# A spectral mixer and token MLP on one core: contiguous chunked filter loads, one product op per unit, the even and odd inverse at once, statistics on two engines

## The chip, the cores and the metric

The kernel runs on one core of a Trainium2 chip. The metric is device time in microseconds (us); lower is better. "Span" is the time from the first to the last instruction in a profile; it is about 1.7 us shorter than the time. A run is called slow when it lies over 1.5% above the fastest of the same kernel; comparisons below use fast runs, and where a slow profile is shown the text says so.

## The reference, cut to what matters

```
x: [1, 2048, 512] bf16;  w_r, w_i: [2048, 257];  w1: [2048, 1376];  w2: [1376, 2048]
h  = x + irfft2( rfft2(layernorm(x)) * (w_r + i*w_i) )     # 2D transform over sequence and width
n  = layernorm(layernorm(h))                               # over the width
u  = gelu(n^T w1 + b1)                                     # an MLP over the sequence (token mixing)
y  = h + (u w2 + b2)^T
```

The kernels compute the transforms as matmuls with constant matrices. Stage by stage: statistics of the 16 row tiles of x and scaling of the forward matrix (FS); first forward matmul and its eviction (Y); second and third forward matmul (CS and a PSUM tile); product with the filter (V); two inverse matmuls (PQ, EO and a PSUM tile); sum with x (H); normalisation (HH); first MLP matmul (HH, weights W1); GELU (GT); second MLP matmul (weights W2); output. The filter takes 4.2 MB in the layout that the product needs: 128 partitions hold 32 groups of 257 values for each of w_r and w_i, used in eight units of four groups. Half of the partitions need rows in rising order ("plain"), the other half in falling order ("mirrored").

## The kernel before

A small scheduler in the program orders all operations and derives the semaphore waits. It finds dependencies by memory cells of 32 bytes:

```python
CELL = 32
...
        b = lo + offs * esz
        c = np.unique(np.concatenate([b // CELL, (b + esz - 1) // CELL]))
        quads = range(p0 // 32, (p0 + pn - 1) // 32 + 1)
        return [q * 16384 + int(x) for q in quads for x in c]
```

The filter is loaded in three chunks of groups. A row is 257 x 2 = 514 bytes, so that chunk borders (byte 4112, for example) fall inside a 32-byte cell:

```python
    for g0, g1 in ((0, 8), (8, 16), (16, 32)):
        n = (g1 - g0) * 257
        for w, dram in ((0, A_w_r), (1, A_w_i)):
            d = Wx[w][0:64, g0:g1, :]                                   # plain half, two copies
            dma(..., d, bass.AP(dram.tensor, g0 * 257, [[0, 2], [64 * 257, 32], [1, n]]), ..., outs=[d], prio=28)
            ...                                                         # one more row for group 0, also [[0, 2], ...]
            for comp in range(2):                                       # mirrored half
                d = Wx[w][64 + comp * 32:96 + comp * 32, h0:g1, :]
                dma(..., d, bass.AP(dram.tensor, (64 - h0) * 257, [[64 * 257, 32], [-257, g1 - h0], [1, 257]]), ..., outs=[d], prio=28)
```

The product takes two VectorE ops of 1024 elements per unit, one for each filter part. The last inverse matmul builds even plus odd and even minus odd in PSUM with three matmuls (512 + 256 + 256 columns), and one VectorE op adds x:

```python
        mm(f"g3_{s2}_e", ..., IF[:, s2, 0, :], ev2, unit, True, False, True, 8, 512, ...)
        for h in range(2):
            mm(f"g3_{s2}_o{h}", ..., IF[:, s2, h, :], EO[:, s2, 256:512], unit, False, h == 1, False, 8, 256)
        K.op(f"h_{s2}", "dve", ... tensor_tensor(hs, ps[:, bank, :], xs, ALU.add) ...)
```

Statistics are VectorE's (`bn_stats` and `bn_aggr`, 16 tiles for each of two normalisations), the scaling of the forward matrix is shared by Pool and ScalarE, and the GELU is a chain of six ops over ScalarE and VectorE.

## Time and profile before

| | us |
|---|---|
| time, median of 3 runs (range) | 206.91 (206.56 to 207.19) |
| start to last forward eviction Y | 0 to 25.4 |
| second forward matmul, filter wait, products, to the start of the inverse | 25.4 to 109.3 |
| inverse and first MLP matmul | 109.3 to 162.6 |
| second MLP matmul, output, end | 162.6 to 205.2 |

The page of the profile cuts the span into 40 slices of 5.1 us. A digit is the busy share of an engine in tenths (9 is 90% or more); PEclk is the granted clock of TensorE in tenths; GB/s is what the DMA engines moved. Then follows the chain of waits, traced back from the last instruction:

```profile
PE   0087599100000000058858999999999999999992
PEclk9999969855555555558997999999999999999999
DMA  5931511414999332326997000000000001211111
GB/s 170 364 159 48 127 51 58 115 46 136 309 412 431 71 90 69 82 55 195 353 285 272 2 0 0 3 0 0 0 2 3 0 26 54 74 53 53 51 51 53
...
PE 44%; SPq 35%; DVE 8%; DMA 8%; issue 2%; ACT 1%; DVEq 0%
PE ps L521 44%; SPq L516 35%; DMA Wi<-in_A_w_i_dram 8%; DVE V L665 7%; DVE OUT L755 0%; ACT U_58 L739 0%; ACT SG_61 L745 0%; ACT PQ L527 0%; SPq L515 0%; DVE Q_59 L741 0%; DVE P_60 L744 0%; DVE GT L747 0%; DVE Q_59 L742 0%; DVEq L421 0%
```

TensorE has nothing to do for nine slices. In six of these the DMA engines are mostly idle too, at 46 to 136 GB/s; in the three between (309, 412 and 431 GB/s) they are full. SPq L516 in the chain is SyncE issuing loads. The timeline of TensorE shows the hole exactly (start, length, instruction, and in brackets the idle time before it):

```profile
36.88 0.61 PE L521 MATMUL ps<-CS,EM 64*128 64x256 bf16 x8 [0.57 <-ACT CS L527]
82.78 0.37 PE L521 MATMUL ps<-EM,V 128*128 128x128 bf16 x2 [45.29 <-DVE V L665]
89.34 1.68 PE L521 MATMUL ps<-EM,V 128*128 128x128 bf16 x14 [6.19 <-DVE V L665]
```

The windows view gives busy time per engine in chosen stretches, then the clock, the DMA share and GB/s (a share can pass 1, because the view counts a packet wholly in the stretch where it starts):

```profile
core 0: us, PE busy (x) PEld busy (x) DVE busy (x) ACT busy (x) POOL busy (x), PEclk, DMA share, GB/s
30.00:33.00 3.00, 3.00 (x30) 2.31 (x29) 0.00 (x0) 2.77 (x5) 0.00 (x0) 1.00 0.12 52
41.00:48.00 7.00, 0.00 (x0) 0.00 (x0) 0.00 (x0) 0.00 (x0) 0.00 (x0) 0.50 0.13 48
60.00:65.00 5.00, 0.00 (x0) 0.00 (x0) 0.00 (x0) 0.00 (x0) 0.00 (x0) 0.50 1.01 425
```

A DMA share of 0.12 to 0.13 is what two of sixteen engines would give (2/16 = 0.125). The packets in the trace fit: from 41 to 48 us nearly all bytes go in packets of 8224 bytes that take 311 ns (median), so that two engines would carry 53 GB/s, beside 48 measured; two packets are in flight for 97% of that stretch, against 16 for 87% of the stretch from 60 to 65 us. (The packed trace does not name the engine of a packet: "two engines" below is read from these numbers.) The timeline of SyncE shows in which order it issued, and how long an issue held it:

```profile
22.31 15.52 SPq L516 DMA_DIRECT2D Wi<-in_A_w_i_dram  x3
37.87 10.72 SPq L516 DMA_DIRECT2D IF<-c_IF  x1
48.64 2.18 SPq L516 DMA_DIRECT2D W_77<-in_B_w_dram  x4
50.86 0.44 SPq L515 DMA_DIRECT2D B1s<-in_B_b_dram  x1
51.34 18.63 SPq L516 DMA_DIRECT2D B2s<-in_B_b_dram  x1
70.01 3.43 SPq L516 DMA_DIRECT2D Wr<-in_A_w_r_dram  x3
...
87.61 0.81 SPq L516 DMA_DIRECT2D Wi<-in_A_w_i_dram  x2
```

The filter rows of the first unit are partly among those issued at 70 us, behind the inverse matrix (IF) and all first MLP weights (W_77): 6.6 MB.

### The profile page before, as it was taken

To read this page: it belongs to the slowest core of one execution; us is meant where nothing else is said; L and a number is where in the kernel's file an instruction comes from. 1 tells how busy PE (TensorE), PEld (TensorE's weight loads), DVE (VectorE), ACT (ScalarE), POOL (GpSimd) and SP (SyncE) were. 2 spreads that over 40 slices of the span, in tenths; PEclk is the share of its full clock that TensorE was granted. 3 is DMA by queue.
4 is the path that set the end of the run, shared out by engine and by line. 5 is a ranking of instruction groups with operands and counts; after the bars stand their busy time and mean duration, and the time that the engine had idled before them with its cause. 6 is when DMAs were issued, how large, how long until landed. Compare 5 with 4: busy or idle time off the path is not lost.

```text
span 205.2 us, 2060 instructions
## 1 busy us (share of the span) xinstructions
PE 129.1 (63%) x775; PEld 77.8 (38%) x784; DVE 87.8 (43%) x199; ACT 72.0 (35%) x128; POOL 7.8 (4%) x14
## 2 busy tenths in 40 slices
PE   0087599100000000058858999999999999999992
PEld 0054346000000000036545665544444566666661
DVE  2787000000000001169992999996885442223321
ACT  2269969400000000024445897646963310000000
POOL 0056200000000000000000000000000000000000
PEclk9999969855555555558997999999999999999999
DMA  5931511414999332326997000000000001211111
GB/s 170 364 159 48 127 51 58 115 46 136 309 412 431 71 90 69 82 55 195 353 285 272 2 0 0 3 0 0 0 2 3 0 26 54 74 53 53 51 51 53
DMA packets 11834, 22.18 MB, mean 108 GB/s; under 512 B 2384, under 2 KB 8528, under 8 KB 11056
## 3 DMA queue, kind: packets, MB, share of 16 engines
q1 hardware_dynamic: 11824, 22.05, 32.4%
q8 instruction: 6, 0.10, 0.2%
q14 instruction: 4, 0.03, 0.0%
HBM read 19.95 MB, written 2.10 MB: 107 GB/s over the span
## 4 chain that ended last, share of the span: by engine, by line
PE 44%; SPq 35%; DVE 8%; DMA 8%; issue 2%; ACT 1%; DVEq 0%
PE ps L521 44%; SPq L516 35%; DMA Wi<-in_A_w_i_dram 8%; DVE V L665 7%; DVE OUT L755 0%; ACT U_58 L739 0%; ACT SG_61 L745 0%; ACT PQ L527 0%; SPq L515 0%; DVE Q_59 L741 0%; DVE P_60 L744 0%; DVE GT L747 0%; DVE Q_59 L742 0%; DVEq L421 0%
## 5 line engine op out<-in xcount | busy, mean ns | idle before, releaser
L521 PE MATMUL ps<-EM,V 128*128 128x128 bf16 x128 | 12.7, 247 | 55.2 <-DVE V L665 54.5
L521 PE MATMUL ps<-HH,W_77 128*128 128x512 bf16 (+1 forms) x171 | 39.9, 379 | 0.3
L521 PEld LDWEIGHTS ps<-EM,V 128*128 128x128 bf16 x128 | 9.2, 111 | 59.2 <-issue 46.2
L527 ACT ACTIVATE PQ<-ps 128x512 bf16<-128x512 f32 x16 | 8.9, 596 | 62.3 <-PE ps L521 62.0
L521 PEld LDWEIGHTS ps<-HH,W_77 128*128 128x128 bf16 (+1 forms) x176 | 17.4, 100 | 18.0 <-ACT HH L593 0.5
L727 DVE CAST B2f<-B2s 128x16 f32<-128x16 bf16 x1 | 0.2, 174 | 53.6 <-DMA B2s<-in_B_b_dram 53.6
L755 DVE SCALAR_TENSOR_TENSOR OUT<-ps,B2f,H 128x512 bf16<-128x512 f32 x16 | 12.0, 751 | 24.2 <-PE ps L521 24.2
L521 PE MATMUL ps<-FS,X 128*128 128x256 bf16 x64 | 10.1, 316 | 13.6 <-POOL FS L610 12.7
L521 PEld LDWEIGHTS ps<-FS,X 128*128 128x128 bf16 x64 | 6.7, 113 | 16.7 <-POOL FS L610 13.5
L665 DVE TENSOR_TENSOR V<-ps,Wi 128x1024 bf16<-128x1024 f32 x8 | 9.8, 1225 | 6.7 <-DMA Wi<-in_A_w_i_dram 6.4
L579 DVE BATCH_NORM_STATS2 st_93<-X 128x6 f32<-128x512 bf16 x16 | 10.5, 671 | 5.0 <-DMA X<-in_A_x_dram 5.0
L715 DVE TENSOR_TENSOR H<-ps,X 128x512 bf16<-128x512 f32 x16 | 10.6, 662 | 4.4 <-PE ps L521 4.4
L665 DVE TENSOR_TENSOR V<-ps,Wr 128x1024 bf16<-128x1024 f32 x8 | 9.7, 1216 | 6.1 <-DMA Wr<-in_A_w_r_dram 6.1
L579 DVE BATCH_NORM_STATS2 st_98<-H 128x6 f32<-128x512 bf16 x16 | 11.0, 690 | 0.2
L527 ACT ACTIVATE CS<-ps 128x512 bf16<-128x512 f32 x16 | 10.3, 791 | 2.3 <-PE ps L521 2.1
L521 PE MATMUL ps<-EM,Y 128*128 128x256 bf16 x64 | 10.0, 302 | 1.4 <-ACT Y L527 1.4
L593 ACT ACTIVATE HH<-H,nb_102,rs_101 128x512 bf16<-128x512 bf16 x12 | 9.7, 811 | 3.3 <-DVE nb_102 L591 3.3
L527 ACT ACTIVATE EO<-ps 128x512 bf16<-128x512 f32 x16 | 9.2, 588 | 2.9 <-PE ps L521 2.7
L521 PE MATMUL ps<-EM,PQ 128*128 128x256 bf16 x64 | 9.7, 289 | 0.7 <-ACT PQ L527 0.7
L521 PE MATMUL ps<-EO,IF 128*128 128x256 bf16 (+1 forms) x48 | 9.6, 308 | 0.1
L527 ACT ACTIVATE Y<-ps 128x1024 bf16<-128x1024 f32 x8 | 7.9, 1022 | 1.8 <-PE ps L521 1.7
L610 POOL TENSOR_SCALAR FS<-FP,rs_96 128x256 bf16<-128x256 bf16 x8 | 7.4, 924 | 14.2 <-ACT FP L598 9.3
(71 smaller groups left out, 177.9 us busy)
## 6 DMA issues: line engine op xcount, KB each, us to landing
W_77<-in_B_w_dram SPq DMA_DIRECT2D x4, 1376.0 KB, 18.8
out_dram<-OUT SPq DMA_DIRECT2D x16, 128.0 KB, 1.8
X<-in_A_x_dram SPq DMA_DIRECT2D x3, 512.0 KB, 8.2
Wr<-in_A_w_r_dram SPq DMA_DIRECT2D x4, 257.0 KB, 21.5
Wi<-in_A_w_i_dram SPq DMA_DIRECT2D x4, 257.0 KB, 22.7
IF<-c_IF SPq DMA_DIRECT2D x1, 1024.0 KB, 21.9
EM<-c_EM SPq DMA_DIRECT2D x1, 768.0 KB, 10.3
Wr<-in_A_w_r_dram SPq DMA_DIRECT2D x1, 514.0 KB
```

Of the source, the lines that this page charges most:

```text
L516: return eng.dma_start(dst, src)
L521: return eng.matmul(outf(bank), lhsT, rhs, start=start, stop=stop, **({"skip_group_check": True} if skip else {}))
L527: return eng.activation(dst, srcf(bank), ACT.Copy)
L579: K.op(f"ln{which}_st{i}", "dve", lambda s, eng, bank: eng.bn_stats(st[:, i, 0:6], src), ins=[src], outs=[st[:, i, 0:6]], dur=680.0, prio= ...
L593: K.op(f"ln{which}_ap{i}", "act", lambda s, eng, bank: eng.activation(dst, src, ACT.Identity, bias=c, scale=b), ins=[src, b, c], outs=[dst ...
L610: return eng.tensor_scalar(FS[:, :, i, :], FP[:, :, i, :], rs, None, op0=ALU.mult)
L665: return eng.tensor_tensor(ov, src, wv, ALU.mult)
L715: K.op(f"h_{s2}", "dve", lambda s, eng, bank, xs=xs, hs=hs: eng.tensor_tensor(hs, ps[:, bank, :], xs, ALU.add), ins=[xs], outs=[hs], dur=6 ...
L727: K.op("b2f", "dve", lambda s, eng, bank: eng.tensor_copy(B2f[:, :], B2s[:, :]), ins=[B2s[:, :]], outs=[B2f[:, :]], dur=80.0)
L755: K.op(f"fin{s2}", "dve", lambda s, eng, bank, dst=dst, bia=bia, hs=hs: eng.scalar_tensor_tensor(dst, ps[:, bank, :], bia, hs, op0=ALU.add ...
```

## The change

The intent: load the filter in five chunks in the order of use, each load with 32 rows outermost; do the product of a unit in one op; let one inverse matmul give even and odd parts and form sum and difference on VectorE; give ScalarE a part of the statistics; use ScalarE's own GELU. The core of the diff, cut:

```diff
-CELL = 32
+CELL = 4
 ...
-    for g0, g1 in ((0, 8), (8, 16), (16, 32)):
-            dma(f"ld_w{w}p_{g0}", d, bass.AP(dram.tensor, g0 * 257, [[0, 2], [64 * 257, 32], [1, n]]), 64 * n * 2, outs=[d], prio=28)
+    for ch, (u0, u1) in enumerate(((0, 1), (1, 2), (2, 4), (4, 6), (6, 8))):
+                d = W[comp::4, g0:g0 + ng, w, :]          # every fourth partition; no outs, the product waits by after=wload[u]
+                lst.append(dma(f"ld_wp{ch}_{w}{comp}", d, bass.AP(dram.tensor, g0 * LW, [[64 * LW, 32], [LW, ng], [1, LW]]), ...
 ...
-        for w in range(2):                                 # two products of 1024 per unit
+            s = bass.AP(s.tensor, s.offset, [list(s.ap[0]), [256, 4], [0, 2], [1, 256]])   # one of 2048, PSUM read twice
+            return eng.tensor_tensor(vout, s, win, ALU.mult)
 ...
-        mm(f"g3_{s2}_e", ...); for h in range(2): mm(f"g3_{s2}_o{h}", ...)
+        mm(f"g3_{s2}", lambda bank: ps[:, bank, :], IF[:, s2, :], EO[:, s2, :], unit, True, True, True, 8, 512)
+        dve(f"tl_{s2}", ... tt[:, 0, :] = ps[256:512] + xl); dve(f"th_{s2}", ... tt[:, 1, :] = xh - ps[256:512])
+        dve(f"h_{s2}", ... hs = ps[0:256] (read twice) + tt)
 ...
+STAT_ACT = (3, 7, 10, 13)                                  # tiles whose statistics ScalarE computes with accumulators
+FS_ACT = (13, 14, 15)                                      # tiles that ScalarE scales, Pool the other 13
 ...
-        gelu{t}_u, _q, _p, _in, _sg, _g                    # six ops
+        act(f"gelu{t}", GT[0:Mt, t, :], ..., ACT.Gelu_apprx_tanh, ...)
```

Also: forward evictions of 512 instead of 1024 elements, the second normalisation with ScalarE's Square and an accumulator, loads of the forward matrix from ScalarE's queue, and a final wait on two stores' semaphores instead of all.

## The prediction

> **What bounds the kernel now.** One hole. In the timeline TensorE does nothing from 37.5 to 82.8 us and little until 91.4 us; in the chain of waits that stretch belongs to SyncE's DMA issues (35% of the span) and to the load of Wi (8%). The windows view gives the reason: from 30 to 33 us and from 41 to 48 us the DMA engines are 12-13% busy and move 48-52 GB/s, while at 60-65 us the same engines move 425 GB/s. 12.5% is 2 of 16 engines. The filter loads that start with a copy dimension of 2, `[[0,2],[64*257,32],[1,n]]`, run then.[...] Dependencies between neighbouring chunks add a second wait (SyncE issues held until 69.97 us, again until 87.6 us). After it the stages are close to their engines: product stage 91.4-107.1 us, VectorE at 2.37 us per unit; inverse plus first MLP matmul 109.3-162.6 us, TensorE back to back; second MLP matmul to 201.3 us, TensorE back to back.
>
> **What the change does, by stage.**
> 1. Start until the first transform is evicted: 24.5 us now. VectorE statistics fall from 16 to 12 tiles (0.67+0.18 us each), ACT gets four, sixteen single reciprocal roots (about 0.29 us) and 16 evictions of 512 instead of 8 of 1024. Pool scales 13 tiles x 0.92 us = 12 us plus small ops, from about 5.5 us. Both engines end near 21-24 us. Estimate 22.5: two us gained.
> 2. Filter loads: the broadcast goes; every load has 32 rows outermost. 514-byte rows already move in the trace on all engines with high throughput when alone (20-25 us). 4.2 MB in 44 loads at 0.43-0.45 us per issue: all issued by 25 us, landed before 30 us. The hole, about 54 us from 37.5 to 91.4, disappears entirely.
> 3. Middle: 8 product ops of 2048 elements, estimated from 1220 ns per 1024 as 2.2-2.3 us, against 2.37 for the pair. ACT (CS 0.79 to 0.60 us, PQ 0.60) and TensorE need almost as much per unit. About 23 us with ramps: 22.5 to 45.5 us.
> 4. Inverse: g3 halves from 1024 to 512 columns, 0.215 us x 16 = 3.4 us of TensorE. VectorE per tile stays about the same (two half adds 0.40, one 0.66, one 0.41, replacing 0.66+0.69+0.18+0.15+scaling). VectorE and TensorE both near 1.7 us per tile. 53.3 becomes about 51.
> 5. GELU as one ACT op: now the chain costs only 3.2 us at its end and TensorE fills it with early second matmuls (0.2 us gap). Gain under 0.5 us.
> 6. Second matmul, stores: unchanged, 42 us.
>
> Sum: 22.5 + 23 + 51 + 42 = 138.5 span, plus 1.7 between span and time, plus about 3 for imperfect overlap: **143 us** (137 to 152). Nearly all of the 64 us is the hole; about 5 us the rest. Faster by over 2%: 0.98; within 2%: 0.01; slower: 0.01.
>
> **What would show it.** No stretch with DMA at 12%; product ops back to back with no wait on W; TensorE's longest idle under 4 us; product op near 2.25 us; g3 16 matmuls; ACT busy up to about 80 us; only two or three ACT table loads; first MLP weights landed by 45 us.
>
> **What would make it wrong.** Square, Abs_reciprocal_sqrt and Copy in different table sets: a load (1.28 us in the trace) per switch would add tens of us. Filter rows at half rate (61 ns instead of 28 in contention would still fit). A TensorE clock at half (it reads 0.5 in idle stretches) for longer at stage borders. ACT as the bottleneck of the first two stages.

The sum came to 138.5 us of span and 143 us of time. That the copy dimension is what holds the loads on two engines was inference from the shares of 12 to 13%.

## The result, and the profile after

The time is 145.22 us median (144.4 to 147.92, 4 runs) beside 206.74 us before (206.11 to 207.19). The ratio of fast runs is 0.7031, with a 95% interval of 0.6975 to 0.7087. A ratio here is the mean time of one kernel's fast runs over that of the other's of the same rounds, so it is not quite the ratio of the medians quoted.

The page of the kernel after (this profile fell in a slow run of 147.92 us; slices are 3.7 us):

```profile
PE   0087952999996589899999999999999999999991
PEclk9999996599999857999999999999999999999999
DMA  3999478888999999997000000000011212121211
GB/s 91 380 403 310 96 175 197 208 184 226 371 411 428 404 204 410 415 318 237 9 0 0 4 0 0 0 0 0 0 40 36 72 36 74 36 72 40 72 41 67
...
PE 59%; DVE 19%; ACT 15%; DMA 3%; POOL 1%; issue 1%
```

The hole is gone: after the first matmuls there is no empty slice for TensorE, and the chain of waits holds DMA with 3% and no issues of SyncE by name. The product no longer waits for the filter. The waits view names who waited for whom (us in total, times, longest):

```profile
DVE V L678 <- PE ps L517: 9.7, 2, 7.7
```

and the windows view, with the same columns, answers the first two rows shown of before:

```profile
30.00:33.00 3.00, 3.00 (x32) 1.38 (x28) 2.73 (x2) 1.76 (x4) 0.00 (x0) 1.00 0.78 174
41.00:48.00 7.00, 5.34 (x74) 4.13 (x75) 7.00 (x5) 4.76 (x9) 0.00 (x0) 1.00 1.02 424
```

SyncE now issues the filter's 44 loads one after the other:

```profile
4.24 3.92 SPq L507 DMA_DIRECT2D W<-in_A_w_r_dram  x6
...
30.87 2.58 SPq L507 DMA_DIRECT2D W<-in_A_w_i_dram  x4
```

Each takes about 0.61 us, the last was issued at 33.4 us, and the last filter rows landed at 36.1 us. The DMA engines were not full meanwhile (the share of 0.78 above), but no product waited for a filter row. Whether a faster issue would have brought the rows earlier is not shown: in b_split_exact below all filter loads were issued by 25.4 us, and the last rows landed at 38.3 us.

The stages of a fast run of the same kernel (the profile of the run a_same below, time 146.59 us, so 0.9 to 2.2 us longer than the three fast runs above):

| stage | before | after | predicted |
|---|---|---|---|
| to the last forward eviction | 25.4 | 26.1 | 22.5 |
| to the start of the inverse | 83.9 | 26.7 | 23 |
| inverse and first MLP matmul | 53.3 | 50.8 | 51 |
| second MLP matmul to the end | 42.6 | 41.2 | 42 |
| span | 205.2 | 144.8 | 138.5 + 3 |

### The profile page after: what moved, and what is told of

Same layout as the page of the kernel before. It is cut to its first block, busy times and chain, and to the rows that moved or that the text cites. A ratio compares the mean times of both kernels' runs of the same rounds, so it can differ in the third digit from the quotient of the medians.

```text
span 146.1 us, 1971 instructions
## 1 busy us (share of the span) xinstructions
PE 124.9 (85%) x752; PEld 73.9 (51%) x752; DVE 64.8 (44%) x116; ACT 69.3 (47%) x160; POOL 14.8 (10%) x34
## 2 busy tenths in 40 slices
DMA packets 16761, 22.17 MB, mean 152 GB/s; under 512 B 2960, under 2 KB 13200, under 8 KB 16240
## 4 chain that ended last, share of the span: by engine, by line
PE 59%; DVE 19%; ACT 15%; DMA 3%; POOL 1%; issue 1%
PE ps L517 59%; ACT Y L535 5%; DVE H L733 5%; DVE V L678 5%; ACT JK L535 4%; DVE HH L738 3%; DMA X<-in_A_x_dram 3%; DVE TT L724 3%; DVE TT L726 2%; ACT EO L535 2%; ACT rs L535 2%; ACT FS L535 1%; DVE st L613 1%; POOL FS L598 1%; DVE OUT L763 1%
## 5 line engine op out<-in xcount | busy, mean ns | idle before, releaser
L517 PE MATMUL ps<-HH,W 128*128 128x512 bf16 (+1 forms) x176 | 40.8, 379 | 0.9 <-DVE HH L738 0.7
L517 PE MATMUL ps<-GT,W 128*128 128x512 bf16 (+1 forms) x176 | 38.2, 379 | 0.0
L517 PEld LDWEIGHTS ps<-GT,W 128*128 128x128 bf16 (+1 forms) x176 | 25.4, 144 | 12.7
L517 PEld LDWEIGHTS ps<-HH,W 128*128 128x128 bf16 (+1 forms) x176 | 17.2, 100 | 21.1 <-DVE HH L738 2.1
L678 DVE TENSOR_TENSOR V<-ps,W 128x2048 bf16<-128x2048 f32 x8 | 17.8, 2282 | 9.7 <-PE ps L517 9.7
L535 ACT ACTIVATE GT<-ps,B1f 128x512 bf16<-128x512 f32 (+1 forms) x11 | 7.1, 689 | 14.6 <-PE ps L517 14.6
L535 ACT ACTIVATE JK<-H,nm 128x512 bf16<-128x512 bf16 x16 | 11.6, 724 | 3.0 <-DVE H L733 2.9
L598 POOL TENSOR_SCALAR FS<-FP,rs 128x256 bf16<-128x256 bf16 x13 | 11.9, 931 | 0.5 <-ACT rs L535 0.5
L733 DVE TENSOR_TENSOR H<-ps,TT 128x512 bf16<-128x512 f32 x16 | 10.9, 681 | 0.0
L613 DVE BATCH_NORM_STATS2 st<-X 128x6 f32<-128x512 bf16 x12 | 7.7, 672 | 5.8 <-DMA X<-in_A_x_dram 5.8
## 6 DMA issues: line engine op xcount, KB each, us to landing
W<-in_A_w_r_dram SPq DMA_DIRECT2D x12, 128.5 KB, 3.0
W<-in_A_w_i_dram SPq DMA_DIRECT2D x12, 128.5 KB, 3.0
```

What stands on the lines that cost most here:

```text
L517: return K.op(name, "pe", lambda eng, bank: eng.matmul(outf(bank), lhsT, rhs, start=start, stop=stop), ins=ins or [lhsT, rhs], occ=occ, la ...
L535: return eng.activation(dst, s, func, **kw)
L598: dve(f"fs{i}", lambda eng, bank: eng.tensor_scalar(FS[:, i, :, :], FP[:, i, :, :], rs, None, op0=ALU.mult), [FP[:, i, :, :], rs], [FS[:, ...
L613: dve(f"st_{i}", lambda eng, bank, i=i, x=x: eng.bn_stats(ST[:, i, 0:6], x), [x], [ST[:, i, 0:6]], 512, prio=25)
L678: return eng.tensor_tensor(vout, s, win, ALU.mult)
L733: return eng.tensor_tensor(hs.rearrange("p (h d) -> p h d", h=2), e, tt[:, :, :], ALU.add)
```

## The experiments

Three sets, the first on one chip and the other two on another, each with the kernel before as partner (medians of 207.35, 207.5 and 207.62 us). All twelve runs gave correct results. In the first set four of the partner's seven runs are slow, one of them with 276.11 us; the partner's three fast runs there have a mean of 205.7 us.

### Set 1: what filled the hole?

The theory after comparing the traces: there are two causes. Loads with a copy dimension of two run on two engines (a DMA share of 0.12 to 0.13); and the false dependencies at chunk borders put the first unit's rows behind 6.6 MB of other loads. The rivals: only one of the two counts, or the rest of the change carries a large share.

**b_split**: the kernel before, the copy loads split in two.

```diff
-            d = Wx[w][0:64, g0:g1, :]
-            dma(..., bass.AP(dram.tensor, g0 * 257, [[0, 2], [64 * 257, 32], [1, n]]), ...)
+            for c in range(2):
+                d = Wx[w][32 * c:32 * c + 32, g0:g1, :]
+                dma(..., bass.AP(dram.tensor, g0 * 257, [[64 * 257, 32], [1, n]]), ...)
```
(and the same for the single row of group 0)

> The kernel before, with one edit: each filter load that began with a copy dimension of 2 becomes two loads of 32 rows, so that it can use all 16 engines. The dependencies between neighbouring chunks, and with them the order of issue, stay. Theory (two causes: two engines, and the order that the false dependencies force, which puts the rows needed first behind the inverse matrix and the first MLP weights, 6.6 MB): about 165 us (158 to 172); no stretch with DMA at 12-13%, but the first product op starts only near 44 us because its mirrored rows are issued after the 6.6 MB. Rival (the two engines are the whole of it): about 150 us, products from about 28 us. Other rival (the order is the whole of it): over 195 us.

Measured: 172.09 us (171.85 to 173.77), ratio 0.8385 (0.829 to 0.8481). The DMA engines are nearly full now up to 44 us (a share of 0.99 from 0 to 26 us, where the kernel before has 0.52, and of 0.94 from 41 to 44 us), but the products begin only at 52.4 us, and they wait for filter rows:

```profile
52.38 1.22 DVE L667 TENSOR_TENSOR V<-ps,Wr 128x1024 bf16<-128x1024 f32 x1 [1.61 <-DMA Wr<-in_A_w_r_dram]
53.94 1.23 DVE L667 TENSOR_TENSOR V<-ps,Wi 128x1024 bf16<-128x1024 f32 x1 [0.34 <-DMA Wi<-in_A_w_i_dram]
```

The theory holds in kind, and its number is missed by a hair (158 to 172 expected): products were expected from 44 us and came 8 us later. The first unit's mirrored rows were issued from 45.3 us on, after SyncE had spent 20.5 us on the issue of a 4 KB load behind the weights.

**b_exact**: the kernel before, with exact dependency cells.

```diff
-CELL = 32
+CELL = 2
-        return [q * 16384 + int(x) for q in quads for x in c]
+        return [q * (1 << 18) + int(x) for q in quads for x in c]
```

> The kernel before, with one edit: the dependency tracker works on cells of 2 bytes instead of 32, so that neighbouring filter chunks no longer wait for each other and are issued in the order of use. The loads with the copy dimension stay on two engines. Theory (two causes): about 166 us (158 to 176); DMA at 12-13% for about 40 us in total, the products of the last four units wait for filter rows until about 55 us. Rival (engines are the whole): over 190 us. Other rival (order is the whole): about 150 us.

Measured: 185.03 us (184.5 to 185.87), ratio 0.9001 (0.891 to 0.9092). The products start at 26.8 us, but the later units wait for filter rows:

```profile
56.53 1.22 DVE L665 TENSOR_TENSOR V<-ps,Wr 128x1024 bf16<-128x1024 f32 x1 [9.96 <-DMA Wr<-in_A_w_r_dram]
72.68 1.23 DVE L665 TENSOR_TENSOR V<-ps,Wi 128x1024 bf16<-128x1024 f32 x1 [14.93 <-DMA Wi<-in_A_w_i_dram]
```

This lies outside the theory's range (158 to 176) and outside both rivals' numbers. The kind is the theory's, the size is not: the last filter rows landed at 72.1 us, not at 55. In the 41 to 48 us window the DMA share is 0.13 with 50 GB/s, as in the kernel before. Where these 17 us come from was not measured.

**b_split_exact**: both edits.

> Both edits together in the kernel before, nothing else of the change. Theory: the hole goes, the products start near 28 us and run on; about 149 us (146 to 153), so that the two edits are not additive (each alone gives about 41 us, both together about 58 us), and everything else in the change is worth about 4 us. Rival (the other parts of the change, such as the single product op, the halved inverse matmul and the split statistics, carry a large share): 155 us or more.

Measured: 151.97 us (151.46 to 153.39), ratio 0.74 (0.7313 to 0.7488). The products run from 27.3 to 48.8 us without a wait for the filter; their waits are for TensorE. The first and the last:

```profile
27.34 1.22 DVE L667 TENSOR_TENSOR V<-ps,Wr 128x1024 bf16<-128x1024 f32 x1 [6.66 <-PE ps L521]
...
47.57 1.22 DVE L667 TENSOR_TENSOR V<-ps,Wi 128x1024 bf16<-128x1024 f32 x1
```

So the loads alone are worth 53.5 us, which is (1 - 0.74) x 205.7, from fast runs alone. The edits alone gave 33.2 and 20.5 us, so that they add up within the noise, which the expectation had denied: I read this as each removing a different part of the delay. The rest of the change is worth what lies between the ratios 0.740 and 0.703, that is 0.037 x 206 = 7.6 us (on this chip, with the two fast runs of a_two below, 7.2 us), against "about 4" expected here and "about 5" in the prediction. A part of this is no merit of the change: the inverse stage of b_split_exact takes 56.6 us where the kernel before needs 53.3. VectorE sits there for 6.8 us before a cast that waits for a small bias load (B1s), and the first sum with x follows only at 56.0 us; in the kernel after, Pool does these casts.

**a_two**: an attempt to put two engines back into the kernel after.

```diff
-bass.AP(dram.tensor, g0 * LW, [[64 * LW, 32], [LW, ng], [1, LW]])
+bass.AP(dram.tensor, g0 * LW, [[16 * 64 * LW, 2], [64 * LW, 16], [LW, ng], [1, LW]])
```

> The kernel after, with one edit: the unmirrored half of the filter loads gets a source whose outermost dimension is 2 (two blocks of 16 rows) instead of 32; the same bytes, rows, number of loads and order of issue. Theory: [...]2.1 MB in 514-byte packets of 28 ns on two engines is about 57 us, products wait for filter rows until about 75 us, time about 178 us (168 to 190). Rival (the count of engines does not matter, only the row shape, the order and the other parts do): 145 to 148 us.

Measured: 146.13 us (144.44 to 147.65, two of the four runs slow, so without a ratio). This experiment failed as such and decides nothing: two evenly spaced blocks of 16 rows are the same pattern as 32 rows, and in the traces the loads are the same as those of the kernel after (44 filter loads of about 0.6 us each, 16,761 packets in all). It serves as another measurement of the kernel after on this chip. The loads that begin with a copy dimension are tested by b_split against before and by b_split_exact against b_exact (185.03 to 151.97 us), where the same rows go in the same order of chunks. Both take away the step of zero together with the count of two. That the count is what matters rests on the share of 0.13 and the packets above; no run separates the two. That any outermost dimension of two puts a load on two engines was not shown.

### Set 2: the first stage and the inverse

In the profile of a_same the kernel after lost 3.6 us to the prediction in the first stage and 3.7 us in the second. The timelines of ScalarE and TensorE in the fast profile a_same:

```profile
16.98 0.90 ACT L535 ACTIVATE FS<-FP,rs 128x256 bf16<-128x256 bf16 x2
17.78 3.98 ACT L535 ACTIVATE Y<-ps 128x512 bf16<-128x512 f32 x8
21.60 0.68 ACT L535 ACTIVATE JK<-X 128x512 bf16<-128x512 bf16 x1
22.12 0.25 ACT L535 ACTIVATION_READ_ACCUMULATOR JK<-X 128x1 f32 x1
22.59 0.72 ACT L535 ACTIVATE JK<-X,nm 128x512 bf16<-128x512 bf16 x1 [0.22 <-DVE nm L607]
...
23.76 0.51 ACT L535 ACTIVATE FS<-FP,rs 128x256 bf16<-128x256 bf16 x1
```

```profile
20.05 0.60 PE L517 MATMUL ps<-FS,X 128*128 128x256 bf16 x4 [0.38 <-POOL FS L598]
24.32 1.04 PE L517 MATMUL ps<-FS,X 128*128 128x256 bf16 x4 [3.68 <-ACT FS L535]
25.62 3.23 PE L517 MATMUL ps<-EM,Y 128*128 128x256 bf16 x14 [0.26 <-ACT Y L535]
```

JK<-X is the statistics of tile 13. In ScalarE's fixed order they stand behind eight evictions, so its scaling (FS at 23.76 us) comes last of all, and TensorE idles 3.68 us before it. VectorE, which computed these statistics before, is idle from about 16 us on. After the pause TensorE's clock is at half: in the clock's record from 23.3 to 30.1 us, and the four matmuls after the pause take 1.04 us where the four before it took 0.60. Only 1.0 and 0.5 occur in the clock's records of the kernels before and after; the half stretches that begin and end within the span last 3.4, 54.6 and 3.4 us before, and 6.8 us twice after. Equal programs differ from run to run by up to 3.4 us (a_same), and there the mean clock differs with the time: of the six runs of a_same the one with 0.976 took 144.53 us, the four with 0.965 took 146.51 to 146.76 us and the one with 0.951 took 147.96 us. (The six runs of a_stat0 below all show a full clock, 1.0, and lie within 0.35 us of each other.) Why the half stretches lie differently from run to run is not shown.

**a_stat3**, a mend of this: `STAT_ACT = (3, 7, 10)` in place of `(3, 7, 10, 13)`, beside **a_same**, the kernel after unchanged.

> The kernel after, unchanged, as the base line of this set: 145 us (144 to 147).

> The kernel after with the statistics of tile 13 moved back from ScalarE to VectorE (three tiles on ScalarE instead of four). Theory (ScalarE's fixed order is the limit of the first stage: the statistics of tile 13 stand behind eight evictions, so the scaled matrix of that tile comes only at 24.2 us, TensorE idles 3.7 us before it[...]): last forward eviction near 22.5 us instead of 26.0, time 141 us (139.5 to 143.5). Rival (sharing the statistics is a gain, or the stage is bound by Pool's 13 scalings): 145 to 147 us, no change.

Measured: a_same 146.65 us (144.53 to 147.96), ratio 0.707 (0.7016 to 0.7125); a_stat3 139.5 us (139.31 to 141.0), ratio 0.6773 (0.6732 to 0.6814). One number in one tuple makes the kernel after 0.6773/0.707 = 0.958 of its time, over 4% faster. The last forward eviction ends at 23.2 us, and the middle stage gains still more (22.9 in place of 26.7 us): TensorE's clock is full there (1.00 from 23.2 to 46.1 us, beside 0.88 in a_same's middle stage), and VectorE's eight products run in one row:

```profile
25.88 18.30 DVE L678 TENSOR_TENSOR V<-ps,W 128x2048 bf16<-128x2048 f32 x8 [9.34 <-PE ps L517]
```

In a_same they came in two groups, later:

```profile
30.51 6.69 DVE L678 TENSOR_TENSOR V<-ps,W 128x2048 bf16<-128x2048 f32 x3 [7.96 <-PE ps L517]
39.19 11.08 DVE L678 TENSOR_TENSOR V<-ps,W 128x2048 bf16<-128x2048 f32 x5 [1.99 <-PE ps L517]
```

The stages of a_stat3 are 23.2, 22.9, 50.2 and 41.2 us: close to the predicted 22.5, 23, 51 and 42. The span, 137.5 us, is 1.0 us under what the prediction had summed before its allowance of 3 us. The edit changes three things at once: the late scaling goes, the half clock after it goes, and the scheduler orders the second stage's operations differently. Other runs give the size of two of them. s3_same below is the same program with a half clock of 3.4 us at this border, and is 1.7 us slower. In a_stat0 and c1 the clock is full (a mean of 1.0 in both profiled runs) and the products still come in two groups, with 19.6 and 20.0 us from first to last in place of 18.3 (19.8 in a_same): the order alone costs about 1.5 us.

**a_stat0**: `STAT_ACT = ()`, all statistics of the first stage on VectorE.

> The kernel after with all statistics on VectorE, as in the kernel before. Theory (ScalarE is the crowded engine in this stage): as fast as the run with three tiles or faster, 140.5 us (138.5 to 143); VectorE's sixteen tiles end near 19 us. Rival (two engines for the statistics are a gain): 147 us or more.

Measured: 140.37 us (140.16 to 140.51), ratio 0.6793 (0.6765 to 0.6821). The rival falls: sharing the statistics of the first stage over two engines gains nothing that these runs resolve (0.6793 against 0.6773, with overlapping intervals), and in the form of the change it costs over 4%.

**a_g3**: the kernel after with the inverse as before: three matmuls (1024 columns) and one add per tile.

```diff
-        mm(f"g3_{s2}", lambda bank: ps[:, bank, :], IF[:, s2, :], EO[:, s2, :], unit, True, True, True, 8, 512)
-        dve(f"tl_{s2}", ...); dve(f"th_{s2}", ...); dve(f"h_{s2}", hadd, ...)
+        mm(f"g3_{s2}_e", ..., IF[:, s2, 0, :], ev2, unit, True, False, True, 8, 512, ...)
+        for h in range(2):
+            mm(f"g3_{s2}_o{h}", ..., IF[:, s2, h, :], EO[:, s2, 256:512], unit, False, h == 1, False, 8, 256)
+        dve(f"h_{s2}", ... tensor_tensor(hs, ps[:, bank, :], xs, ALU.add) ...)
```

> The kernel after with the inverse as in the kernel before: three matmuls of 1024 columns per tile and one add, instead of one of 512 and three adds. Theory (TensorE bounds this stage from 61 us on, without gaps): 0.215 us x 16 = 3.4 us longer, 148 us (146.5 to 149.5), although VectorE then needs 0.9 instead of 1.6 us per tile. Rival (the chain of waits, which runs over VectorE from 63 to 82 us, names the limit): 142 to 145 us.

Measured: 150.49 us (150.11 to 154.03), ratio 0.7289 (0.7245 to 0.7334) against 0.707, which is 0.022 x 207.5 = 4.5 us longer; expected were 3.4, and 150.49 lies outside the range given. TensorE bounds this stage (busy for 49.6 of 50.8 us in a_same) although the chain of waits runs over VectorE there in the kernel after. I read the longer chain entry as VectorE keeping pace, not as the limit: halving TensorE's work for one matmul was worth it, though VectorE does three adds for one. The excess of 1.1 us over the sum is within the two intervals (together about 3 to 6 us). Part of it may lie elsewhere: the inverse matrix is 0.5 MB larger in this run, and the schedule of the first stage changed with it. Only slow profiles can be set side by side here (this run's of 154.03 us and the one of the kernel after): in these the inverse stage takes 55.5 against 52.3 us, which fits the 3.4, and the first stage 29.1 against 26.0 us.

### Set 3: the product op, the GELU, and an attempt at more

The base line is a_stat3 again, as **s3_same**.

> The version with three tiles of statistics on ScalarE again, as the base line of this set: 139.5 us (139 to 141).

Measured: 141.06 us (139.32 to 142.69), ratio 0.6773 (0.6732 to 0.6814), as in set 2. Its single runs form two groups, and the profile, of a run of 141.03 us, shows why: in the clock's record the half stretch is at 23.5 to 26.9 us, at the start of the second stage, and not at 14.9 to 18.4 us as in a_stat3 (a run of 139.31 us).

```profile
27.57 18.30 DVE L678 TENSOR_TENSOR V<-ps,W 128x2048 bf16<-128x2048 f32 x8 [10.90 <-PE ps L517]
```

The row of products is the same 18.30 us, but starts 1.7 us later (27.57 against 25.88), and the two times differ by 1.7 us too.

**s3_v2**: two product ops of 1024 per unit in this base.

```diff
-            return eng.tensor_tensor(vout, s, win, ALU.mult)        # one op, [256, 4], [0, 2], [1, 256]
+        for w in range(2):                                          # two ops, V[:, g0:g0 + 4, w, :]
+            ... eng.tensor_tensor(vout, psf[...].rearrange("p (g l) -> p g l", g=4), win, ALU.mult)
```

> The base of this set with the product in two ops of 1024 elements per unit, as in the kernel before, instead of one of 2048. Theory (VectorE bounds the middle stage; the pair took 2.37 us from start to start, the single op 2.22): 8 x 0.15 = 1.2 us longer, 140.7 us (140 to 141.5). Rival (ScalarE and TensorE bind the middle stage as much): no difference, under 0.4 us.

Measured: 142.44 us (141.65 to 144.81), ratio 0.6851 (0.6807 to 0.6894): 0.0078 x 207.6 = 1.6 us more than the base, though the intervals touch. The products take 20.7 us in place of 18.3:

```profile
27.52 4.62 DVE L678 TENSOR_TENSOR V<-ps,W 128x1024 bf16<-128x1024 f32 x4 [10.89 <-PE ps L517]
32.59 2.36 DVE L678 TENSOR_TENSOR V<-ps,W 128x1024 bf16<-128x1024 f32 x2 [0.45 <-PE ps L517]
35.46 2.36 DVE L678 TENSOR_TENSOR V<-ps,W 128x1024 bf16<-128x1024 f32 x2 [0.52 <-PE ps L517]
```

The 142.44 us lie outside the range expected (140 to 141.5). Only a part of the longer row is the op itself: eight pairs of 2.36 us are 18.9. The other part is waits for TensorE between the pairs. So the theory holds in sign; in the trace the waits around the pair cost more (1.8 us) than the pair itself (0.6 us).

**s3_gelu**: the six-op GELU of the kernel before in this base.

> The base of this set with the GELU of the kernel before (six ops over ScalarE and VectorE) instead of one. Theory (TensorE fills the chain's end with second matmuls that need only earlier tiles): up to 0.8 us longer. Rival (the five ops removed per tile shorten the critical path): 2 us longer or more.

Measured: 141.03 us (140.86 to 141.29), ratio 0.6791 (0.6761 to 0.6821). No difference from the base that the runs resolve. In the chain of waits from 90 to 110 us there is only TensorE: it works on second matmuls that need earlier tiles while the last tile passes through the six ops. Removing five ops per tile bought nothing here.

**c1**: two of Pool's scalings and four of ScalarE's evictions moved to VectorE.

```diff
+FS_DVE = (9, 12)
-Y_DVE = ()
+Y_DVE = ((4, 1), (5, 1), (6, 1), (7, 1))
```

> An attempt at a faster version: the base of this set with two of Pool's 13 scalings (tiles 9 and 12) and four of ScalarE's sixteen forward evictions (the last four of one half) moved to VectorE, which idles from 16.5 to 25.9 us. Theory (Pool's row of eight scalings up to 19.8 us and ScalarE's row of ten evictions up to 23.2 us end the first stage): last forward eviction at 20.5 to 21.5 us instead of 23.2, time 137 us (136 to 138.5). Rival (something else holds the second stage): 139 us or more.

Measured: 139.93 us (139.34 to 140.95), ratio 0.675 (0.6709 to 0.6791). This misses its expectation of 137 us (136 to 138.5), and the rival's number stands. The first stage ends at 21.5 us instead of 23.3 (s3_same) and the products start at 24.25 us, but the gain is given back:

```profile
24.25 6.69 DVE L682 TENSOR_TENSOR V<-ps,W 128x2048 bf16<-128x2048 f32 x3 [3.36 <-PE ps L518]
33.12 11.08 DVE L682 TENSOR_TENSOR V<-ps,W 128x2048 bf16<-128x2048 f32 x5 [2.19 <-PE ps L518]
```

After three products VectorE waits 2.19 us for TensorE, and the last product ends at 44.2 us as in a_stat3. The two groups are those of a_same: with these edits the scheduler again puts the second stage's operations in the less lucky order. The best time that I can vouch for is therefore that of a_stat3 and c1, 139.3 us in their faster runs, about 4% below the kernel after; the two are not told apart.

## Why the prediction was right

The prediction said 143 us (137 to 152); 145.22 was measured. Point by point:

1. **The hole.** Right: it disappeared, with no DMA share of 0.12 left before the stores. The attribution was only half right. The prediction put the hole down to the copy dimension and called the dependencies "a second wait". The runs show two causes, neither of which is a detail: 33.2 us for the copy dimension alone, 20.5 us for the dependencies alone, 53.5 for both. Had the change kept the dependencies and only cured the copy dimension, the prediction's reasoning would have been off by some 20 us. In b_split the same bytes in loads of 32 rows took the DMA share from 0.52 to 0.99 (0 to 26 us).
2. **Filter landing.** "All issued by 25 us, landed before 30" was wrong: issued by 33.4 and landed at 36.1 us. An issue took 0.61 us and not 0.43 to 0.45, but that was not the whole error. In b_split_exact the filter loads were issued by 25.4 us and landed by 38.3, with the engines full at 178 to 200 GB/s (16 to 36 us; a share of 0.99 from 0 to 26 us). The prediction had judged the rows' throughput from 20 to 25 us of the trace before, where the share was only 0.54 (its second half, from 22.5 us on, had 0.87 and 183 GB/s). It cost nothing, since no product waited for a filter row. The first MLP weights landed at 53.9 us and not by 45; their first use was at 61 us.
3. **First stage.** 22.5 us predicted, 26.1 measured. This is the term that was mis-sized most, together with the next. I had added up the work of ScalarE and Pool and not followed ScalarE's fixed order. The prediction's list of dangers had the cause, "ACT as the bottleneck of the first two stages". a_stat3 gives 23.2 us.
4. **Middle stage.** 23 us predicted, 26.7 measured, and 22.9 in a_stat3 where the clock is full. The half clock at a stage border was in the list of dangers, too; it was not in the sum, only in the 3 us of allowance. The single product op is 2.28 us, as estimated (2.2 to 2.3).
5. **Inverse.** 51 predicted, 50.8 measured. The mechanism is TensorE's: undoing the halved matmul costs 4.5 us (3.4 estimated, as 16 x 0.215 us per 512 columns; in the second MLP stage of the kernel after 176 matmuls of 512 columns are busy for 38.2 us, 0.217 us each).
6. **GELU.** Under 0.5 us predicted; the runs show no difference.
7. **Second matmul.** 42 predicted, 41.2 measured. The final wait on two semaphores instead of all is part of the difference as far as the traces can tell: the last store landed 1.4 us before the end of the span before, and 0.4 us after.

So the total was right because the hole was sized rightly, and because an allowance of 3 us covered part of the 7 us that the first two stages lost in a_same. The allowance was made for imperfect overlap and not for this late item, so that this part is luck.

## What to carry to other kernels

Look at the DMA share in the stretch where everything waits: here a share of 0.12 to 0.13 (2/16) with nobody else busy belonged to loads whose outermost dimension was a copy dimension of two, and splitting these took it to 0.99 (b_split, 0 to 26 us). Then look at the order in which the loads were issued: a dependency tracker with cells coarser than the data's borders can put the first rows needed behind megabytes that nobody needs yet, and such a second cause may hide behind the first. When work is moved to a less busy engine, follow that engine's fixed order, not its sum: one late item there stopped TensorE for 3.7 us, and its clock was at half for 6.8 us around that pause's end (a_same).

## What else the traces show

- TensorE's clock dropped after stretches in which TensorE was partly busy. In the 3.4 us before a drop there were 0.60 us of matmuls (drop at 23.3 us, a_same), 1.25 us (50.6 us, a_same), 1.66 us (14.9 us, a_stat3), 0.89 and 1.27 us (22.7 and 50.1 us, the kernel after), and 1.57, 1.22 and 1.49 us (25.5, 39.1 and 107.4 us, the kernel before). It stayed full after 3.4 us with 2.67 and with 2.91 us of matmuls (a_same). What decides is not shown.
- A single filter load of the kernel after landed soon after its issue (3.0 us, the median of the 128.5 KB loads). But for 44 loads at 0.61 us SyncE issued for 29 us, from 4.2 to 33.4 us, and the DMA engines were not full (0.78 from 30 to 33 us). What that cost is not shown (b_split_exact issued faster and landed later). The shortest issues of filter loads took 0.31 to 0.45 us in the kernel before, whose rows go into neighbouring partitions, and 0.60 us in the kernel after, where they go into every fourth. Whether the partition step is the cause was not isolated.
- Single issues lasted far longer behind other loads: 10.72 and 18.63 us in the kernel before and 12.54 us in the kernel after, the last two for the same 4 KB load. That full queues are the reason is inferred from what was in flight, not shown.
- ScalarE's accumulator output has a cost of its own: the trace shows a separate instruction of 0.19 us after each (24 in the kernel after), so that the statistics of tile 13 with their root held ScalarE for about 1.9 us (21.60 to 23.72 us in a_same, less 0.22 us idle). ScalarE's table loads took 1.28 us each, two in the kernel before and two in the kernel after.
